# Three x tiles instead of four turned on TensorE, the fourth by the crossbar, and the gate weights loaded as five rows

## The chip, the cores and the metric

The kernel runs on one core of a Trainium2 chip. The time is device microseconds of that core. Each run lists a granted clock of 1.0 (1.0 is TensorE's full speed); that figure does not show the stretch at half speed that is found below (the page of before has 9, its top digit, in all 40 slices of that clock, and the first of them, 6.5 us long, holds the matmuls up to 3.7 us, which ran at half speed). A single profiled execution has a span 1.2 to 1.6 us shorter than the time that is quoted for it, because the time also holds what lies outside the profile.

## The reference, cut to what matters

```python
# x (2048, 640), wqkv (640, 1920), gate_w (640,)
g = sigmoid((x * gate_w).sum(-1, keepdims=True))
a = linear_attention(x @ wqkv) @ wo          # phi(q), phi(k): phi(t) = where(t > 0, t+1, exp(t)) + 1e-6
b = mixer_mlp(layernorm(x), w1, w2, w3, w4)
return g * a + (1 - g) * b
```

Only the first 20 us matter here: x comes in as 16 tiles of 128 tokens, each is turned (its features, in five slices of 128, become its rows) before TensorE multiplies it by the query and key weights, and `gate_w` rides along as one more column of the key weights, so that the gate's dot product costs no instruction of its own.

## The kernel before

The first four tiles are turned by TensorE (`t_x`, five 128x128 transposes each, then a copy on VectorE out of PSUM, the `ps` of the traces, into which TensorE writes). Tiles 4 to 15 are turned by a DMA that transposes on its way (DMA_TRANSPOSE in the traces; "through the crossbar" is its name here), which the SP queue issues after it has waited for the tile's 640 KB load. Query and key products come in "steps": one k (one of the five slices of 128 features) of one tile, a 512-column and a 128-column matmul.

```python
    dma_in(x_tok[:, 0, :], ...); dma_in(x_tok[:, 1, :], ...)      # cut
    load_wq(0)
    dma_in(x_tok[:, 2:4, :], x2[256:512, :]..., "x23")
    for k in range(1, KD): load_wq(k)
    for k in range(KD): dma_in(wkg[:, k, 0:D], ..., "wk%d" % k)
    dma_in(wkg[:, :, D + 2:D + 3], gate_w.rearrange("(k p o) -> p k o", p=128, o=1), "gw", noncontig=True)
    for c in range(1, NCH):
        dma_in(x_tok[:, 4 * c:4 * c + 4, :], ..., "xc%d" % c)
        for t in range(4 * c, 4 * c + 4):
            sch.dma("sp", xT[:, :, 128 * t:128 * (t + 1)], x_tok[:, t, :], "trx%d" % (t % 4), transpose=True)
    # ...
    WARM = 3200
    def t_x(t):
        tr_group(b, [x_tok[:, t, 128 * k:128 * (k + 1)] for k in range(KD)])   # cut: bank, src, dst
        copy(dve, dst, src)
    # ...
    def q_four():       # (tile, k); (tile, None) is t_x; (None, None) a short warm-up
        order = [(0, 0), (None, None), (1, 0), (2, None), (3, None), (0, 1), (1, 1), (2, 0), ...]
    # then k_first for tile 0, key tiles 1 to 3, and q, k of tile 4, 5, ...
```

A warm-up of 3,200 columns of matmul on a block of ones runs on TensorE while the first loads are under way.

## Time and profile before

| what | value |
|---|---|
| time | 260.96 us median of 3 (260.87 to 261.06) |
| TensorE (PE) busy | 255.7 of 259.6 us |
| PE's waits in all, after the first matmul | 0.8 us |
| first query step / first key step / query 4 | 5.06 / 11.80 / 17.27 us |
| crossbar transpose of tile 4 landed | 15.85 us |

From the page of before, the busy times, the granted clock in 40 slices, and the chain that ended last:

```profile
PE 255.7 (99%) x1690; PEld 132.2 (51%) x1690; DVE 151.7 (58%) x287; ACT 106.8 (41%) x216; POOL 92.8 (36%) x152
...
PEclk9999999999999999999999999999999999999999
...
PE 97%; DMA 1%; DVE 0%; SPq 0%; issue 0%
```

The whole kernel is one long stream of matmuls. Almost nothing is waited for, so what can be gained is TensorE work or one of the early waits. The early stretch is in the timeline of before (columns: start, busy time, engine, line, operation, tiles, count, and in brackets the idle time and what ended it):

```profile
3.69 0.75 PE L611 MATMUL ps<-ident,x_tok 128*128 128x128 bf16 x10
...
5.06 0.39 PE L874 MATMUL ps<-wq,xT 128*128 128x512 bf16 x1 [0.51 <-DMA wq<-in_A_wqkv_dram]
...
5.91 0.73 PE L611 MATMUL ps<-ident,x_tok 128*128 128x128 bf16 x10
6.48 0.38 PE L874 MATMUL ps<-wq,xT 128*128 128x512 bf16 x1
...
11.10 0.38 PE L874 MATMUL ps<-wq,xT 128*128 128x512 bf16 x1
11.31 0.22 PE L875 MATMUL ps<-wq,xT 128*128 128x128 bf16 x1
11.80 0.38 PE L874 MATMUL ps<-wkg,xT 128*128 128x512 bf16 x1 [0.27 <-issue]
```

Ten transposes take 0.57 us from the first to the next matmul (5.91 to 6.48). A query step takes 0.272 us, so the last one, started at 11.10, lets the next start at 11.37; the first key step starts at 11.80. The view says "issue", but the program makes this matmul wait for the gate load too. SP's timeline and the list of DMA issues (KB each, us to landing) give that load:

```profile
6.96 0.43 SPq L284 DMA_DIRECT2D wkg<-in_gate_w_dram  x1
wkg<-in_gate_w_dram SPq DMA_DIRECT2D x1, 1.2 KB, 4.7
```

Issued at 6.96, 4.7 us to landing: 11.7 us, for 1.2 KB. It came as 640 packets of 2 bytes, which started between 9.1 and 11.4 us, beside and behind the key weights.

### The profile page before, as it was taken

What the parts mean: (1) busy time and instruction counts of PE and PEld (TensorE: products, weight loads), DVE (VectorE), ACT (ScalarE), POOL (GpSimd) and SP (SyncE); (2) the same over time, 40 slices, a digit from 0 to 9 for tenths busy, and PEclk for the clock granted to TensorE, in tenths of its full rate; (3) what the DMA queues carried; (4) which work ended last, traced back from release to release, by engine and by line L of the source; (5) the groups of instructions that cost most, each with busy time, mean ns of one, the idle gap of its engine ahead of it and who ended that gap; (6) DMA issues with size and microseconds to landing.
All of it is one profiled execution on the core that took longest, in us unless ns stands there. A gap on an engine that the chain in (4) does not pass through costs nothing.

```text
span 259.6 us, 4300 instructions
## 1 busy us (share of the span) xinstructions
PE 255.7 (99%) x1690; PEld 132.2 (51%) x1690; DVE 151.7 (58%) x287; ACT 106.8 (41%) x216; POOL 92.8 (36%) x152
## 2 busy tenths in 40 slices
PE   7999999999999999999999999999999999999996
PEld 4555555554445454554444545554455544456453
DVE  1587887899902799999998407993033410143233
ACT  1496677751355766685854240005500045200000
POOL 4003995969863019667903202230011110021001
PEclk9999999999999999999999999999999999999999
DMA  6845969572656991752726650232000020000211
GB/s 195 260 104 146 198 176 143 167 139 44 110 108 123 352 337 36 72 101 52 105 56 124 124 61 0 41 85 78 0 3 0 3 101 0 0 3 1 104 51 51
DMA packets 51348, 24.99 MB, mean 96 GB/s; under 512 B 42708, under 2 KB 49917, under 8 KB 51328
## 3 DMA queue, kind: packets, MB, share of 16 engines
q1 hardware_dynamic: 49952, 21.31, 35.2%
q0 software_dynamic: 1136, 3.28, 5.8%
q8 instruction: 13, 0.21, 0.4%
q10 hardware_dynamic: 240, 0.13, 0.2%
q14 instruction: 7, 0.06, 0.1%
HBM read 12.05 MB, written 2.62 MB: 57 GB/s over the span
## 4 chain that ended last, share of the span: by engine, by line
PE 97%; DMA 1%; DVE 0%; SPq 0%; issue 0%
PE ps L600 61%; PE ps L1152 22%; PE ps L782 8%; PE ps L874 2%; DMA wq<-in_A_wqkv_dram 1%; PE ps L1064 1%; PE ps L1134 1%; PE ps L875 1%; DVE x_tok L639 0%; PE ps L954 0%; PE ps L983 0%; SPq L285 0%; PE ps L611 0%; PE ps L1131 0%; PE ps L847 0%
## 5 line engine op out<-in xcount | busy, mean ns | idle before, releaser
L600 PE MATMUL ps<-xnT,w 128*128 128x512 bf16 x360 | 81.5, 379 | 0.0
L1152 PE MATMUL ps<-w,h2T 128*128 128x512 bf16 (+1 forms) x416 | 58.8, 299 | 0.0
L656 ACT ACTIVATE h2T<-ps 128x512 bf16<-128x512 f32 x52 | 30.5, 598 | 67.5 <-PE ps L600 67.5
L600 PEld LDWEIGHTS ps<-xnT,w 128*128 128x128 bf16 x360 | 34.2, 98 | 38.5 <-issue 0.9
L639 DVE SCALAR_TENSOR_TENSOR x_tok<-ps,stg,abx 128x512 bf16<-128x512 f32 (+1 forms) x32 | 17.3, 550 | 61.5 <-PE ps L1152 61.5
L622 POOL TENSOR_SCALAR abx<-x_tok,stg 128x640 f32<-128x640 bf16 x16 | 14.8, 927 | 99.9 <-DVE x_tok L639 94.9
L1152 PEld LDWEIGHTS ps<-w,h2T 128*128 128x128 bf16 x416 | 32.2, 98 | 24.9 <-issue 1.1
L622 POOL TENSOR_SCALAR xn<-x_tok,st 128x640 bf16<-128x640 bf16 x32 | 34.4, 1082 | 14.3 <-DMA xnT<-xn 13.6
L656 ACT ACTIVATE Er<-ps 128x640 bf16<-128x640 f32 x32 | 22.5, 705 | 17.9 <-PE ps L600 8.5
L655 ACT ACTIVATE junk<-x_tok 128x640 bf16<-128x640 bf16 x32 | 23.6, 737 | 3.1 <-DVE x_tok L637 2.6
L600 PE MATMUL ps<-M_sb,pqnT 128*128 128x512 bf16 (+1 forms) x160 | 24.3, 299 | 0.0
L656 ACT ACTIVATE hsT<-ps 128x512 bf16<-128x512 f32 (+1 forms) x32 | 18.9, 594 | 13.0 <-PE ps L600 12.6
L600 PE MATMUL ps<-w,hsT 128*128 128x512 bf16 (+1 forms) x160 | 23.7, 299 | 0.0
L600 PE MATMUL ps<-wkg,xT 128*128 128x512 bf16 (+1 forms) x150 | 22.6, 299 | 0.0
L639 DVE SCALAR_TENSOR_TENSOR abx<-ps,stg,abx 128x640 f32<-128x640 f32 x16 | 14.1, 884 | 12.7 <-PE ps L600 11.7
L600 PEld LDWEIGHTS ps<-w,hsT 128*128 128x128 bf16 x160 | 13.3, 98 | 12.2
L600 PEld LDWEIGHTS ps<-M_sb,pqnT 128*128 128x128 bf16 x160 | 13.2, 98 | 10.9
L600 PE MATMUL ps<-wq,xT 128*128 128x512 bf16 (+1 forms) x120 | 18.3, 299 | 0.0
L782 PE MATMUL ps<-pk_tok,x_tok 128*128 128x512 bf16 x80 | 17.8, 379 | 0.0
L622 DVE TENSOR_SCALAR Er<-Er 128x640 bf16<-128x640 bf16 x32 | 11.6, 363 | 9.6 <-ACT Er L656 9.2
L637 DVE SCALAR_TENSOR_TENSOR x_tok<-ps,x_tok 128x640 bf16<-128x640 f32 x16 | 13.1, 820 | 6.4 <-PE ps L600 5.9
L600 PEld LDWEIGHTS ps<-wkg,xT 128*128 128x128 bf16 x150 | 12.2, 98 | 9.0
(75 smaller groups left out, 231.2 us busy)
## 6 DMA issues: line engine op xcount, KB each, us to landing
w<-in_B_w_dram SPq DMA_DIRECT2D x1, 2160.0 KB, 9.6
w<-in_B_w_dram SPq DMA_DIRECT2D x1, 2080.0 KB, 15.2
x_tok<-in_A_x_dram SPq DMA_DIRECT2D x3, 640.0 KB, 5.9
out_dram<-x_tok SPq DMA_DIRECT2D x3, 640.0 KB, 3.1
w<-in_B_w_dram POOLq DMA_DIRECT2D x8, 160.0 KB, 4.5
wq<-in_A_wqkv_dram SPq DMA_DIRECT2D x5, 160.0 KB, 3.6
wkg<-in_A_wqkv_dram SPq DMA_DIRECT2D x5, 160.0 KB, 4.3
wv<-in_A_wqkv_dram POOLq DMA_DIRECT2D x1, 800.0 KB, 5.9
```

Source lines behind the costliest of these rows:

```text
L600: ins = e.matmul(out_ap, l, r, start=(i == 0), stop=(i == n - 1))
L622: return engf(lambda e: e.tensor_scalar(out_ap, in_ap, s1, s2, op0, op1), rd, [out_ap], cost=cost)
L637: return dve(lambda e: e.scalar_tensor_tensor(out_ap, in0, scalar, in1, op0, op1, accum_out=accum), rd, [out_ap, accum], cost=cost + 70.0)
L639: return dve(lambda e: e.scalar_tensor_tensor(out_ap, in0, scalar, in1, op0, op1), rd, [out_ap], cost=cost)
L655: return act(lambda e: e.activation(out_ap, in_ap, func, bias=bias, scale=scale, accum_out=accum), rd, wr, cost=cost)
L656: return act(lambda e: e.activation(out_ap, in_ap, func, bias=bias, scale=scale), rd, wr, cost=cost)
L782: ins = e.matmul(o, l, r, start=(t0 + q_ == 0), stop=(t0 + q_ == NT - 1))
L874: e.matmul(ps[:, b, 0:512], l, w[:, k, 0:512], start=(k == 0), stop=(k == KD - 1))
L875: return e.matmul(ps[:, b + 1, 0:n2], l, w[:, k, 512:512 + n2], start=(k == 0), stop=(k == KD - 1))
L1064: ins = e.matmul(o, l, r, start=st, stop=sp)
L1134: ins = e.matmul(ps[:, bm, :], l, w4[rows, KFF, 0:512], start=True, stop=False)
L1152: ins = e.matmul(o, l, r, start=False, stop=(i == KFF - 1), skip_group_check=(n0 > 0))
```

## The change

The intent: take five transposes from TensorE (tile 3 goes through the crossbar, behind the keys of tiles 0 to 2), and bring `gate_w` in as five rows of 256 bytes, early and on another queue, into a zeroed 128-row block that one 5-column matmul turns into a column.

```diff
-    dma_in(x_tok[:, 2:4, :], ..., "x23")
+    dma_in(x_tok[:, 2, :], x2[256:384, :], "x2")
     for k in range(KD):
         dma_in(wkg[:, k, 0:D], ..., "wk%d" % k)
-    dma_in(wkg[:, :, D + 2:D + 3], gate_w..., "gw", noncontig=True)
+        if k == 2:
+            dma_in(x_tok[:, 3, :], x2[384:512, :], "x3")
+    gwr = xn[:, 1, 0:128]
+    dve(lambda e: e.memset(gwr, 0.0), [], [gwr])
+    sch.dma("act", xn[0:KD, 1, 0:128], gate_w.rearrange("(k p) -> k p", p=128), "gw")
     for c in range(1, NCH):
         dma_in(x_tok[:, 4 * c:4 * c + 4, :], ..., "xc%d" % c)
-        for t in range(4 * c, 4 * c + 4):
+        for t in range(3 if c == 1 else 4 * c, 4 * c + 4):
             sch.dma("sp", xT[...], x_tok[:, t, :], ..., transpose=True)
...
     def t_x(t):
+        if t == 2:
+            mm_group(ps[:, b, 448:448 + KD], [(gwr, ident[:, 0:KD])])
         copy(dve, dst, src)
+        if t == 2:
+            copy(dve, wkg[:, :, D + 1:D + 2], ps[:, b, 448:448 + KD]...)
...
-    q_four: order = [(0,0), warm, (1,0), tx2, tx3, (0,1), (1,1), (2,0), ...]; then k_first, key tiles 1 to 3
+    q_three: order = [(0,0), warm, (1,0), tx2, (0,1), (1,1), (2,0), ...]; then k_two (tiles 0, 1), key tile 2, query 3, key 3
-    key matmuls of 131 columns (two of ones, one of the gate)
+    key matmuls of 130 columns
```

(One POOL memset moved. From query 4 on the two programs have the same order on every engine.)

More of the change, by code (lines that the diff above doesn't have):

```diff
@@ L683, in _build @@
     load_wq(0)
-    dma_in(x_tok[:, 2:4, :], x2[256:512, :].rearrange("(n p) d -> p n d", p=128), "x23")
+    dma_in(x_tok[:, 2, :], x2[256:384, :], "x2")
     for k in range(1, KD):
@@ L688, in _build @@
         dma_in(wkg[:, k, 0:D], A_wqkv[128 * k:128 * (k + 1), D:2 * D], "wk%d" % k)
-    dma_in(wkg[:, :, D + 2:D + 3], gate_w.rearrange("(k p o) -> p k o", p=128, o=1), "gw", noncontig=True)
+        if k == 2:
[3 more added lines that the diff above has]
+    sch.dma("act", xn[0:KD, 1, 0:128], gate_w.rearrange("(k p) -> k p", p=128), "gw")
     for c in range(1, NCH):
         dma_in(x_tok[:, 4 * c:4 * c + 4, :], x2[512 * c:512 * (c + 1), :].rearrange("(n p) d -> p n d", p=128), "xc%d" % c)
-        for t in range(4 * c, 4 * c + 4):
+        for t in range(3 if c == 1 else 4 * c, 4 * c + 4):
             sch.dma("sp", xT[:, :, 128 * t:128 * (t + 1)], x_tok[:, t, :], "trx%d" % (t % 4), transpose=True)
@@ L727, in _build @@
     memset(pool, ones_c[:], 1.0)
+    memset(pool, wkg[:, :, D:D + 1], 1.0)
     aselect(ident[:], ones_c[:, 0:128], [[-1, 128]], ALU.is_equal, 0, 1)
-    memset(pool, wkg[:, :, D:D + 2], 1.0)
     memset(pool, negh[:], -0.5)
@@ L757, in t_x @@
         dst = xT[:, :, 128 * t:128 * (t + 1)]
+        if t == 2:
+            mm_group(ps[:, b, 448:448 + KD], [(gwr, ident[:, 0:KD])])
         copy(dve, dst, src)
+        if t == 2:
+            copy(dve, wkg[:, :, D + 1:D + 2], ps[:, b, 448:448 + KD].rearrange("p (k o) -> p k o", o=1))
     def phi(b, dst, after_exp=None):
@@ L772, in k_tile @@
         mm_group(ps[:, b, 0:512], [(xT[:, k, tok], wkg[:, k, 0:512]) for k in range(KD)])
-        mm_group(ps[:, b + 1, 0:131], [(xT[:, k, tok], wkg[:, k, 512:D + 3]) for k in range(KD)])
+        mm_group(ps[:, b + 1, 0:130], [(xT[:, k, tok], wkg[:, k, 512:D + 2]) for k in range(KD)])
         k_out(t, b)
@@ L879, in stream, with q_three, k_two @@
                 done(t, b)
-    def q_four():
-        order = [(0, 0), (None, None), (1, 0), (2, None), (3, None), (0, 1), (1, 1), (2, 0), (0, 2), (1, 2), (3, 0), (0, 3), (1, 3), (0, 4),
-                 (2, 1), (1, 4), (2, 2), (2, 3), (2, 4), (3, 1), (3, 2), (3, 3), (3, 4)]
+    def q_three():
+        order = [(0, 0), (None, None), (1, 0), (2, None), (0, 1), (1, 1), (2, 0), (0, 2), (1, 2), (2, 1), (0, 3), (0, 4),
+                 (1, 3), (2, 2), (1, 4), (2, 3), (2, 4)]
         stream(order, wq, 128, lambda t, b: phi(b, pq_tok[:, t + 1, :]))
     def k_out(t, b):
-        k_done[t] = phi(b, pk_tok[:, t, :], lambda: activation(lr[:, t, :], ps[:, b + 1, 129:131], ACTF.Copy))
+        k_done[t] = phi(b, pk_tok[:, t, :], lambda: activation(lr[:, t, :], ps[:, b + 1, 128:130], ACTF.Copy))
         activation(junk[:, 0, :], x_tok[:, t, :], ACTF.Square, accum=st1[:, 1, t:t + 1])
-    def k_first():
-        stream([(0, k) for k in range(KD)], wkg, 131, k_out)
+    def k_two():
+        stream([(0, 0), (0, 1), (0, 2), (1, 0), (0, 3), (1, 1), (1, 2), (0, 4), (1, 3), (1, 4)], wkg, 130, k_out)
     def addA(name, dur, fn, deps=()):
@@ L899, in _build @@
     addA(("warm", 1), 0.0, lambda: warmup(WARM2, 0.42))
-    addA(("q", 3), 5.44, q_four)
-    addA(("k", 0), 1.36, k_first)
-    for i in range(1, 4):
-        addA(("k", i), 1.36, lambda t=i: k_tile(t))
-    for i in range(4, NT + 2):
+    addA(("q", 2), 4.08, q_three)
+    addA(("k", 1), 2.72, k_two)
+    addA(("k", 2), 1.36, lambda: k_tile(2))
+    for i in range(3, NT + 2):
         if i < NT:
@@ L907, in _build @@
             addA(("k", i), 1.36, lambda t=i: k_tile(t))
-        for t in range(3) if i == 4 else (i - 2,):
-            addA(("g0", t), 0.27, lambda t=t: gt_tail(t), deps=[(("k", t), 2.0)])
+        if i > 3:
+            for t in range(3) if i == 4 else (i - 2,):
+                addA(("g0", t), 0.27, lambda t=t: gt_tail(t), deps=[(("k", max(t, 1)), 2.0)])
     IT.add("LW", ("lw1",), 0.0, load_w1, deps=[(("k", 5), 0.0)])
@@ L1231, in _build @@
     for t in range(NT):
-        deps = [(("zb",), 1.0), (("q", max(t, 3)), 2.0)]
+        deps = [(("zb",), 1.0), (("q", max(t, 2)), 2.0)]
         if t < 7:
```

## The prediction

> **What bounds the kernel.** TensorE. The page has PE busy 255.7 of 259.6 us (99%), full granted clock in all 40 slices, and the chain of waits is 97% PE; PE's own waits sum to 1.9 us, all before 12 us. A saving counts only if it shortens TensorE's stream or one of those early waits; then it should last to the end, for after the first few matmul groups both programs have the same order on every engine.
>
> **The early part before (timeline, landings).**
> - Ten transposes of tiles 2 and 3 start at 5.91, as their 320 KB landed at 5.86; PE was free at 5.73. They hold PE 0.57 us (57 ns each).
> - The 18 query steps after them run at 0.272 us each and end at 11.37. The first key matmul starts only at 11.80: 0.43 us lost. The page calls the gap "issue", but that matmul also waits for the gate_w load, which landed at 11.71, 1.08 us after the last key weights (10.63). The packets show why: 640 of 2 bytes between 9.2 and 11.5 us, DMA down to 114 GB/s. [...]
>
> **The change, costed.**
> 1. Five transposes leave PE: -0.285 us.
> 2. The gate load becomes five rows, early, on another queue; keys no longer wait for it: -0.43 us.
> 3. Tile 2 arrives alone, half the bytes: estimate 5.4 instead of 5.86, so its transposes start about 5.74: -0.17 us.
> 4. Key matmuls of 130 columns, not 131, 80 of them at about 0.4 ns a column: -0.03 us.
> 5. Added on PE: one 5-column matmul, about +0.06 us. Memset and 128x5 copy are on an idle DVE.
>
> All lies on PE's chain: -0.85 us if nothing new waits. By this sum queries 0-2 end at 9.65, keys 0-1 at 12.36, key 2 at 13.72, and query 4 starts at 16.4 instead of 17.27 (estimates).
>
> **New waits that may take some back.**
> - wq3 and wq4 landed at 8.05 and 8.46 and are now needed at 7.7 and 8.0. With 160 KB less ahead (0.44 us by the landings' spacing) they come at about 7.6 and 8.0: no slack, estimate 0.1 us lost.
> - Key tile 1 needs query 0's PSUM pair, free at 10.35 by the spacing of before, needed at 10.4.
> - Tile 3's crossbar transpose is issued when x3 lands (about 9.8). [...] it runs behind the 640 KB of tiles 4-7, clear about 12.2. Estimated landing 13.2, needed at 13.7. [...]
>
> I expect 0.15 us of these, net -0.7 us (0.3%): **260.25 us**, 8 in 10 between 259.9 and 260.8. Chances: faster by over 2% 0.005, within 2% 0.99, slower by over 2% 0.005.
>
> **What would show each step.** The first key matmul follows the last query matmul with no idle time (2); five transposes near 5.75 without the idle before them (1, 3); query 4 near 16.5 (sum); PE waits on wq, on the crossbar's xT or on DVE (new waits). From query 4 on everything stands 0.7 us earlier.
>
> **What would make it wrong.** The crossbar transpose landing after 14 us, so that PE waits at query 3 and the gain is gone, or a loss of up to 1 us; the first wq load delayed by the gate load or the later table load on ACT; the shift absorbed by a later wait without slack.

(Cut from the record: two rules about DMA that were quoted, not measured, and a sentence on a straggling DMA engine, which no run shows. No term of the sum is cut: items 1 to 5 still come to -0.85 us, and with 0.15 us of new waits to -0.7. That tile 3's transpose runs behind the 640 KB load, clear about 12.2, and lands at 13.2 thus stands as the author's estimate; in after that load landed at 13.52 and the transpose at 14.27. The 0.4 ns a column of item 4 is the query step's 0.272 us over its 640 columns. The 0.06 us of item 5 names no source; 0.03 was measured, in c2.)

## The result

| | time, us | ratio to before |
|---|---|---|
| before, 6 runs | 260.91 median (260.47 to 261.39) | |
| after, 6 runs | 260.81 median (260.68 to 261.05) | 0.9995 (0.9982 to 1.0008) |
| after again (a1), 5 runs | 261.14 median (260.79 to 261.82) | 1.0006 (0.9991 to 1.0020) |

A ratio here and below is the mean time of one kernel's fast runs over that of the other's of the same rounds, so not quite the ratio of the medians; the brackets are the 95% interval. Of the 0.7 us that was predicted nothing can be told from zero.

Lines of the page of after that answer to those of before:

```profile
PE 254.8 (98%) x1655; PEld 133.0 (51%) x1686; DVE 152.0 (59%) x288; ACT 106.5 (41%) x216; POOL 93.6 (36%) x152
...
PE 98%; issue 1%; DVE 0%; POOL 0%; POOLq 0%
```

Matmul records are missing from this trace (1,655 of 1,686), so the busy time does not say that TensorE worked less. This page has no row for the granted clock at all. The timeline of after over the same stretch:

```profile
3.69 1.27 PE L611 MATMUL ps<-ident,x_tok 128*128 128x128 bf16 x10
...
5.11 0.59 PE L882 MATMUL ps<-wq,xT 128*128 128x512 bf16 x1
...
5.81 0.63 PE L882 MATMUL ps<-wq,xT 128*128 128x512 bf16 x1
...
6.34 0.74 PE L611 MATMUL ps<-ident,x_tok 128*128 128x128 bf16 x5
6.88 0.21 PE L600 MATMUL ps<-ident,xn 128*128 128x5 bf16 x1
6.95 0.38 PE L882 MATMUL ps<-wq,xT 128*128 128x512 bf16 x1
...
7.44 0.22 PE L883 MATMUL ps<-wq,xT 128*128 128x128 bf16 x1
7.70 0.39 PE L882 MATMUL ps<-wq,xT 128*128 128x512 bf16 x1
...
10.64 0.22 PE L883 MATMUL ps<-wq,xT 128*128 128x128 bf16 x1
10.70 0.38 PE L882 MATMUL ps<-wkg,xT 128*128 128x512 bf16 x1
...
17.53 1.52 PE L600 MATMUL ps<-wq,xT 128*128 128x512 bf16 x10
```

Three things are to be seen.

1. The first key step follows the last query step without a gap (10.64, 10.70). That part of the change works as meant.
2. The same ten transposes at 3.69 took 1.27 us instead of 0.75, and the first 512-column query matmuls 0.59 and 0.63 instead of 0.39. From 6.95 on everything is as fast as before. **TensorE ran at half speed until 6.9 us here, and only until 3.7 us in the profile of before.** The starts of successive transposes tell it: 107 ns apart, which is called half speed here, or 56 ns, full speed. In a2 and b3 the change falls within this group of ten, which takes 1.15 and 0.88 us.
3. Between 7.44 and 7.70 a step is 0.2 us late; the view names no cause (b2 and c4 below find it).

The SP timelines of before and then of after show the crossbar transposes (DMA_TRANSPOSE), merged:

```profile
13.38 5.25 SPq L281 DMA_TRANSPOSE xT<-x_tok  x4
```

```profile
9.85 9.57 SPq L281 DMA_TRANSPOSE xT<-x_tok  x5
```

The individual landings, from the trace's landing records: in before tile 4 landed at 15.85, 1.4 us ahead of query 4 at 17.27. In after tile 3 landed at 14.27, and tile 4 at 17.45, 0.08 us ahead of query 4 at 17.53.

So there were two theories. **A**: the moment of full speed is drawn anew in each execution (it was 3.7 us in the profile of before and 6.9 in that of after), and a late draw costs the new kernel what it gained. **B**: tile 4's transpose now lands so late that TensorE could not have started query 4 sooner whatever happened before.

### The profile page after: what moved, and what is told of

Same layout as the page of the kernel before. It is cut to its first block, busy times and chain, and to the rows that moved or that the text cites. A ratio compares the mean times of both kernels' runs of the same rounds, so it can differ in the third digit from the quotient of the medians.

```text
span 259.8 us, 4263 instructions
## 1 busy us (share of the span) xinstructions
PE 254.8 (98%) x1655; PEld 133.0 (51%) x1686; DVE 152.0 (59%) x288; ACT 106.5 (41%) x216; POOL 93.6 (36%) x152
## 4 chain that ended last, share of the span: by engine, by line
PE 98%; issue 1%; DVE 0%; POOL 0%; POOLq 0%
PE ps L600 61%; PE ps L1160 21%; PE ps L790 8%; PE ps L882 2%; PE ps L855 1%; PE ps L1072 1%; PE ps L1142 1%; PE ps L883 1%; PE ps L611 1%; DVE x_tok L639 0%; PE ps L962 0%; PE ps L991 0%; PE ps L1139 0%; POOL xn L659 0%; POOLq L1306 0%
## 5 line engine op out<-in xcount | busy, mean ns | idle before, releaser
L600 PE MATMUL ps<-xnT,w 128*128 128x512 bf16 x348 | 80.4, 379 | 0.7 <-issue 0.2
L600 PE MATMUL ps<-M_sb,pqnT 128*128 128x128 bf16 (+1 forms) x156 | 23.6, 297 | 0.3
L600 PE MATMUL ps<-wkg,xT 128*128 128x130 bf16 (+1 forms) x138 | 21.1, 298 | 0.1
L600 PE MATMUL ps<-wq,xT 128*128 128x128 bf16 (+1 forms) x128 | 19.7, 298 | 0.1
L600 PEld LDWEIGHTS ps<-M_sb,pqnT 128*128 128x128 bf16 x160 | 13.2, 98 | 10.8
L1101 DVE TENSOR_TENSOR pq_tok<-pq_tok,dnr 128x300 bf16<-128x300 bf16 (+1 forms) x48 | 16.8, 403 | 0.6
```

What stands on the lines that cost most here:

```text
L600: ins = e.matmul(out_ap, l, r, start=(i == 0), stop=(i == n - 1))
L1101: dve(lambda e, o=o, i0=i0, i1=i1: e.tensor_tensor(o, i0, i1, ALU.mult), [i0, dnr[:, 1, sd, :]], [o], cost=cost)
```

## The experiments

Twelve kernels ran, all with the right result, in three groups of four; those of one group ran on one chip and share the runs of before; the groups ran on three different chips. From query 4 on nothing differs but one column, so one number of a profile tells the rest: the start of the first product of x with the keys (the "tail product", which follows key 4). Time of the profiled run minus this start lay between 240.79 and 240.97 us in all eleven profiles of this table, so the start is the time up to 0.2 us.

| kernel | full speed from | first key step | waits from there to the tail product | tail product | time of this run |
|---|---|---|---|---|---|
| before | 3.74 | 11.80 | 0 | 20.00 | 260.84 |
| a2, before again | 4.58 | 11.50 | 0 | 19.70 | 260.57 |
| b4, before, early warm-up | 5.5 | 11.47 | 0 | 19.67 | 260.64 |
| a3, gate part alone | 3.73 | 11.98 | 0 | 20.16 | 261.01 |
| c2, gate part, early warm-up | 5.6 | 11.61 | 0 | 19.79 | 260.59 |
| after | 6.9 | 10.70 | 0 | 20.25 | 261.05 |
| a1, after again | 6.9 | 10.69 | 0.79 | 21.03 | 261.82 |
| a4, after, tile 4 loaded alone | 6.9 | 10.70 | 0 | 20.25 | 261.06 |
| c1, after, early warm-up | 4.88 | 9.87 | 0.54 | 19.96 | 260.77 |
| b3, both | 3.97 | 10.06 | 0 | 19.61 | 260.41 |
| c3, both, copy cut in two | 6.8 | 10.39 | 0 | 19.94 | 260.73 |

"Full speed from" is read from the trace's clock record where there is one and else from the spacing of the matmuls. "Waits" is the tail product's start minus that of the first key step, less 8.20 us in the kernels that turn four tiles on TensorE (six tile products and no wait) and less 9.55 in the others (seven). The profiles of b1, b2 and c4 are left out of the table: there time minus this start is 241.17, 241.04 and 241.08.

### a1 and a2: the two kernels again

No edit.

> The changed kernel unaltered, for a second profile and more times. Theory A (the start of full TensorE speed falls at a random time): in the profile of after, matmuls ran at half speed until about 6.9 us, in that of before only until 3.7 us; the moment should differ again here, and the start of query 4 should follow it: near 16.5 if full speed starts before 4.5 us, near 17.5 if after 6.5 us. Theory B (tile 4's crossbar transpose caps the gain): query 4 does not start before its xT lands (17.45 in the profile of after), whatever the speed; with an early full speed TensorE shows an idle gap before query 4 of 0.3 to 1 us.

> The kernel before, unaltered, as a control and for a second profile. Ratio 1.000 within 0.001. Theory A: the first half-speed stretch ends anywhere between 3.6 and 7 us, and a late end puts the start of query 4 up to 1 us later than 17.27. If it is again near 3.7 and the times of both kernels spread alike, theory A does not explain the lost gain.

a1: 261.14 us (260.79 to 261.82), ratio 1.0006. a2: 260.75 (260.57 to 261.45), ratio 0.9998 (0.9984 to 1.0012). In a1 full speed came late again, at 6.9, and this time theory B's wait is in the profile. The list of TensorE's waits and the timeline of a1:

```profile
PE ps L600 <- DMA xT<-x_tok: 0.6, 1, 0.6
```

```profile
16.16 1.53 PE L600 MATMUL ps<-wkg,xT 128*128 128x512 bf16 x10
18.30 1.53 PE L600 MATMUL ps<-wq,xT 128*128 128x512 bf16 x10 [0.61 <-DMA xT<-x_tok]
```

Key 3 would have let query 4 start at 17.52; it started at 18.30, when tile 4's transpose had landed at 18.25. This is the slowest run of the eleven of after. Theory B's wait is shown, and it can come even with a late full speed.

a2 shows something else. Its gate load landed at 11.41 and its first key step started at 11.50:

```profile
11.18 0.22 PE L875 MATMUL ps<-wq,xT 128*128 128x128 bf16 x1
11.50 0.38 PE L874 MATMUL ps<-wkg,xT 128*128 128x512 bf16 x1
```

The query steps alone give 11.24: this gap is 0.26 us, not 0.43. In b4's profile the load landed at 11.19, before the query steps ended, and there is no gap at all.

a2 also limits theory A. Its full speed came 0.84 us later than in before, and yet its query 4 started at 16.97, 0.30 us earlier, not later. The same holds for b4 and c2 (full speed at 5.5 and 5.6, query 4 at 16.94 and 17.06). In before TensorE waited for weights until 5.06 and for tiles 2 and 3 until 5.91, so slow work ahead of those waits need not cost anything. No profile with four tiles on TensorE has a start as late as 6.9.

### a3: the gate part alone

```diff
 (before, with:)
-    dma_in(wkg[:, :, D + 2:D + 3], gate_w..., "gw", noncontig=True)
+    memset of gwr, five rows on the ACT queue, 5-column matmul and 128x5 copy in t_x(2), 130 key columns
```

> Before with only the gate part of the change (five rows, zeroed block, one 5-column matmul, 130 key columns); all four tiles still turned on TensorE. If the 2-byte gate load cost 0.43 us of TensorE time, the first key matmul follows the last query matmul without a gap, and the time is 0.3 to 0.45 us below before (ratio about 0.9985), for the crossbar of tile 4 has slack (landed 15.85, needed 17.27 in before). Rival: the gap is given back in a later wait, ratio 1.000.

261.01 us (260.77 to 261.38), ratio 1.0001 (0.9990 to 1.0013): the expected 0.3 to 0.45 us is not there. The first key step follows the last query step at once, at 11.98. But in this profile tiles 2 and 3 landed at 6.42 instead of 5.86, and the timeline of a3 has the wait one step earlier:

```profile
6.47 0.45 PE L611 MATMUL ps<-ident,x_tok 128*128 128x128 bf16 x5 [0.49 <-DMA x_tok<-in_A_x_dram]
```

The gap before the keys stood in series with other loads that vary by half a microsecond from run to run. That this edit made the load late is not shown: in c2, with the same edit, tiles 2 and 3 landed at 5.92. The rival (the gap is given back in a later wait) is neither shown nor refuted: the loss in this profile came before the gap, not after it.

### a4: tile 4 loaded by its own transfer

```diff
 (after, with:)
+        if c == 1:
+            dma_in(x_tok[:, 4, :], x2[512:640, :], "x4")
+            dma_in(x_tok[:, 5:8, :], x2[640:1024, :]..., "xc1")
```

> After, but tile 4 of x is loaded by its own 160 KB transfer ahead of tiles 5 to 7, so its crossbar transpose need not wait for the whole 640 KB. Theory B: its transpose is issued at about 11.7 instead of 13.5 us, lands near 14.5 instead of 17.45, query 4 starts right behind key 3, and the time drops 0.3 to 0.7 us below after. Theory A alone: no difference from after beyond 0.1 us.

The mechanism did what was expected: tile 4's transpose was issued at 11.18 and landed at 14.24, 3.3 us before it was needed. The time did not move in the median, 260.90 us, but the six runs spread from 260.12 to 262.61 (two of them, 260.12 and 260.23, as fast as b3 below), ratio 0.9999 (0.9974 to 1.0023). The profile explains its own run: full speed only from 6.9, first key at 10.70, no wait after it, query 4 at 17.53, and 261.06 us. So even without theory B's wait the gain is gone in this profile, by the late full speed and by 0.21 us that b2 finds: the cap was not the only thing in the way. The slow outlier and the two fast runs have no profile.

### b1 and b2: all real work held back until full speed is sure

```diff
 (before, and after, with:)
-    memset(pool, ones_c[:], 1.0)
+    for _ in range(8):
+        memset(pool, ones_c[:], 1.0)     # the identity for the transposes comes behind these
-    WARM = 3200
+    WARM = 7168
```

> The kernel before, with all real TensorE work held back to about 7 us by seven more memsets ahead of the identity and 7,168 instead of 3,200 warm-up columns, so that TensorE is at full speed before its first transpose whenever that speed starts (3.7 to 7.0 us). Theory A (the moment of full speed scatters the times): the spread of the times falls from about 0.9 us to under 0.35 us. Time about 2.3 us above before: transposes at 7.05 instead of 3.7, but no wait for any wq, x or gate load afterwards. Rival (scatter comes from elsewhere, such as late loads): spread stays about 0.9 us.

> The changed kernel with the same delay. Query 4 then starts near 20 us, well after tile 4's crossbar transpose (17.5 to 18.3 us), and no load is waited for; what is left of the change is five transposes less on TensorE, one 5-column matmul more, one column less: 0.25 us below b1, to the end of the kernel, with a spread under 0.35 us. If it is not below b1, TensorE time saved here is given back later, which no theory so far says.

b1: 264.33 us, five runs within 264.33 to 264.34. b2: 264.17 us, 264.17 to 264.20. (The work started at 7.75 instead of the expected 7.05, which is 0.7 of the microsecond by which both are longer than expected.) The scatter of 0.9 us and more that before shows beside them (260.69 to 262.23) is gone. That shows that it arises in the first 7.75 us, but not which of the two things the hold-back removes made it: both a late full speed and a late first load are hidden by it. Full speed started at 3.69 in the profile of b1 and at 6.91 in that of b2, with no effect on the work behind.

The second result is a surprise: b2 is 0.16 us faster than b1, not 0.25. The timeline of b1, where every load is long there and full speed reigns, and then those of b2, TensorE's and VectorE's:

```profile
9.52 0.72 PE L611 MATMUL ps<-ident,x_tok 128*128 128x128 bf16 x10
...
10.62 0.38 PE L875 MATMUL ps<-wq,xT 128*128 128x512 bf16 x1
```

```profile
10.10 0.38 PE L883 MATMUL ps<-wq,xT 128*128 128x512 bf16 x1
10.31 0.22 PE L884 MATMUL ps<-wq,xT 128*128 128x128 bf16 x1
10.58 0.39 PE L883 MATMUL ps<-wq,xT 128*128 128x512 bf16 x1
```

```profile
10.03 0.49 DVE L665 COPY xT<-ps 128x640 bf16<-128x640 bf16 x1 [0.91 <-PE ps L600]
```

The step of b2 at 10.58 should have started at 10.37. It is query 2's first, and it needs tile 2's turned x, which VectorE copies out of PSUM after the transposes, here from 10.03 to 10.52. b1's step at 10.62 is the same one, and nothing delays it. In before five more transposes (those of tile 3) stood between the transposes of tile 2 and this step; now only two steps do. In the two profiles the tail product is only 0.04 us apart (23.17 and 23.13). The transposes that were taken away had been covering a copy. From the tail product to the last matmul b2 is another 0.04 us shorter (237.29 to 237.33 us), as step 4's missing column would make it. So TensorE's stream explains about 0.08 of the 0.16 us; the rest lies outside the profiled span (1.59 us in b1, 1.49 in b2) and has no known cause.

### c4: the same with the copy of tile 2 cut in two

```diff
 (b2, with, in t_x:)
-        copy(dve, dst, src)
+        for k0, k1 in ((0, 2), (2, KD)) if t == 2 else ((0, KD),):
+            copy(dve, dst[:, k0:k1, :], src[:, k0:k1, :])
```

> b2 with the same cut copy, where times repeat within 0.03 us. If the removed transposes uncovered the copy, the time drops by 0.15 to 0.21 us from 264.17 to about 264.0, which then is 0.3 us below b1: the TensorE time that the prediction counted. Rival: no change, 264.17.

263.98 us (263.98 to 264.02), 0.19 below b2 and 0.35 below b1. It ran on another chip than those two, so the profile is the firmer witness. The timeline of c4:

```profile
10.11 0.38 PE L884 MATMUL ps<-wq,xT 128*128 128x512 bf16 x1
10.32 0.22 PE L885 MATMUL ps<-wq,xT 128*128 128x128 bf16 x1
10.39 0.39 PE L884 MATMUL ps<-wq,xT 128*128 128x512 bf16 x1
```

The step starts at 10.39 instead of 10.58, and the tail product at 22.94 instead of 23.13: 0.19 us, all of which arrives at the end. The wait was the copy.

### b3 and b4: an earlier warm-up

```diff
 (a4, and before, with:)
-    memset(pool, xn[:, 0, 0:128], 1.0)          # the warm-up's operand
-    WARM = 3200
+    WARM = 3456
-    e.matmul(..., xn[:, 0, 0:128], xn[:, 0, 0:128]...)
+    e.matmul(..., nc.const_aps.tensor(1.0, [128, 128], BF16), nc.const_aps.tensor(1.0, [128, n], BF16))
```

> The x4 split, with the warm-up matmuls on a constant that the preamble has written, so that they start 0.25 us earlier (0.80 instead of 1.05), 256 more columns. [...] Then full speed from about 3.5 us in the profile, query 4 near 16.5 us, and 260.2 us in the median (0.7 below before). Rival: the profile shows half speed until 6.9 us again, and the time is that of the x4 split, 260.9.

> The kernel before with only the earlier warm-up. Its three profiles (this one, a2, a3 family) already had full speed from 3.7 to 4.6 us, so: same as before, ratio 0.9985 to 1.0, fewer runs above 261.3.

b3: 260.34 us (260.14 to 260.85), ratio 0.9968 (0.9950 to 0.9985), clearly faster than before on the same chip. b4: 260.90 (260.55 to 261.40), ratio 0.9987 (0.9971 to 1.0004), not told from before. The warm-up started at 0.83 instead of 1.05. In b3's profile full speed came at 3.97 (3.5 was expected), the first query step had to wait for its weights until 5.33, and no wait followed. Tile 4's transpose landed at 14.49.

```profile
5.33 0.39 PE L885 MATMUL ps<-wq,xT 128*128 128x512 bf16 x1 [0.68 <-DMA wq<-in_A_wqkv_dram]
...
6.00 0.44 PE L611 MATMUL ps<-ident,x_tok 128*128 128x128 bf16 x5
...
10.06 0.38 PE L885 MATMUL ps<-wkg,xT 128*128 128x512 bf16 x1
```

Five transposes take 0.27 us here (6.00 to the next matmul at 6.27) against 0.54 in after. This is about the kernel that was predicted.

### c1, c2, c3: which part of b3 did it

c1 is after with only the earlier warm-up, c2 the gate part (a3) with it, c3 is b3 with the copy cut in two; no edits beyond those shown.

> The changed kernel with only the earlier warm-up, no split of the 640 KB load. Theory B: with full speed by about 4 us TensorE reaches query 4 near 16.5 us but tile 4's crossbar transpose lands at 17.4 to 18.3, so TensorE idles 0.5 to 1.5 us there and the time is 0.4 to 0.8 us above that of c3 or b3 (260.34), that is 260.7 to 261.2. Rival (the early warm-up alone made b3 fast): 260.3, no idle time before query 4.

> Before with the gate part and the earlier warm-up; tile 3 still turned on TensorE, nothing on the crossbar before tile 4. It lacks the removed transposes, but also the new waits. If the gate part is worth what the gap before the first key matmul showed (0.1 to 0.43 us in two profiles of before), it is 0.1 to 0.4 us below b4 (260.9), near 260.6, and above b3.

> b3 with the copy of tile 2's turned x out of PSUM cut in two (k 0 to 1, then 2 to 4), so that query 2's first matmul waits for the first piece only. In after, a1, a4, b2 and b3 that matmul started 0.21 us late behind this copy. Expect the gap gone and about 0.2 us below b3: 260.15, the fastest version, 0.3% below before. Rival: the gap is wq2 or the bank, and the time is b3's.

c1: 260.92 us (260.41 to 261.12), ratio 0.9995 (0.9982 to 1.0007). The time is in theory B's range, but its profile corrects the theory. Full speed came at 4.88 and the first key step at 9.87, 0.83 earlier than in after. Then 0.54 us went, and not to tile 4, which had landed at 16.57. The timeline of c1:

```profile
12.11 0.39 PE L881 MATMUL ps<-wkg,xT 128*128 128x512 bf16 x1 [0.15 <-DMA wkg<-in_A_wqkv_dram]
...
12.94 1.53 PE L600 MATMUL ps<-wkg,xT 128*128 128x512 bf16 x10
14.51 1.53 PE L600 MATMUL ps<-wq,xT 128*128 128x512 bf16 x10
...
17.24 1.03 PE L600 MATMUL ps<-wq,xT 128*128 128x512 bf16 x4
```

The last key weights landed at 12.06, and the step that needs them, which the steps before it allowed at about 11.80, started at 12.11. A key tile takes 1.36 us, so query 3 could have started at 14.30; tile 3's transpose landed at 14.47, and it started at 14.51. So at an early full speed TensorE outran two other loads first. What theory B says of tile 4 holds of the whole queue: key weights 4, tile 3 and tile 4 are all close to TensorE's need.

c2: 260.95 us (260.59 to 261.14), ratio 0.9998 (0.9986 to 1.0011): again nothing for the gate part alone, against the expected 0.1 to 0.4 us.

c3: 260.50 us (260.15 to 260.81), ratio 0.9982 (0.9970 to 0.9995). Faster than before a second time, on another chip, but not faster than b3 as expected. In its profile full speed came only at 6.8, in spite of the earlier warm-up, and still its first key step came at 10.39, 0.31 before that of after. The cut copy's 0.19 us, which c4 shows, is smaller than the scatter of the start.

### What holds the transposes up

Two further things were read in all profiles rather than tried. First, in each one an instruction fetch of 16 KB (a queue of its own, kind "instruction", 13 in the whole kernel) passes once between 13 and 18.2 us. In before and a2 it fell at 13.2 us, ahead of the first crossbar packet, and all four transposes landed 2.5 to 2.6 us after their issue. In after (15.36 us), a1 (14.88), a3 (13.83), a4 (15.78), b1 (16.27), b2 (18.12), b3 (14.16), c3 (14.89) and c4 (17.34) one transpose that was in flight then landed 3.7 to 4.6 us after its issue: about 19 or 20 of its 256-byte packets, which take 18 ns in the median, took from 0.5 to 1.9 us where they were looked at (after, a1, a3, a4). In the remaining three (b4 at 13.26, c2 at 13.56, c1 at 13.87) it began 0.1 to 0.9 us after the issue of tile 4's transpose, which landed 2.8 to 3.3 us after its issue: the same pattern, smaller. Where it fell on tile 4 (after, a1, a3) that tile came late; where tile 4 had been issued earlier (a4, b3, c3) it fell on a later tile that had slack. The coincidence is there in nine profiles, and weaker in three, but no run moved the fetch, so the cause is argued, not shown. Second, tile 3's packets in after and a1 stood up to 1.5 and 1.8 us among those of the 640 KB load, whose landing (13.52 and 13.82) was not earlier than in before (13.36), although the 2-byte packets were gone. The prediction had it clear at 12.2, by an estimate. The order was as predicted (the transpose landed after that load, at 14.27 and 14.57), the times were not.

## Why the prediction was right or wrong

The time lies at the edge of the stated range (260.81, range to 260.8) and "within 2%" is right. Neither credits the mechanism: without any gain the time would have been 260.9, only 0.1 us away, which is less than the runs scatter. The forecast gain of 0.7 us is wrong: six and five runs show none. Point by point:

- **"TensorE bounds the kernel, and a saving lasts to the end": right.** Time minus the start of the tail product is 240.8 to 241.0 us in the eleven profiles of the table (241.0 to 241.2 in b1, b2 and c4), and c4's 0.19 us arrived whole.
- **Step 1, five transposes, -0.285: the work is right, the credit wrong.** Five take 0.27 us at full speed. But "all lies on PE's chain" failed: they had hidden the copy of tile 2, and 0.21 us came back as a wait behind VectorE (b2: the tail product 0.04 us earlier than b1; c4: 0.19 more once the copy is cut). The prediction called that engine idle and did not ask what its latency stood behind.
- **Step 2, the gate load, -0.43: mechanism right, size taken from one profile.** The gap is 0.43, 0.26 and 0 us in three profiles of before (before, a2, b4), and alone it brought nothing that the times show (a3, c2).
- **Step 3, tile 2 alone, 5.4 instead of 5.86: right** (5.25 and 5.47 in after and a1). In those two TensorE was still at half speed then and could not use it.
- **Steps 4 and 5: right, and small.** With 130 columns the stretch from the tail product to the last matmul is 237.29 us, with 131 it is 237.33 in before and b1 (a2 and b4 have further delays there). The 5-column matmul holds TensorE for 0.03 us at full speed (0.06 was predicted): in c2 it starts at 6.28 and the next transpose at 6.31.
- **The sum, first key step at 9.65: nearly right where its premise held.** In c1, with full speed at 4.88, it is 9.87: 9.65 and the 0.21 of the copy. (In b3, with 3.97, it is 10.06, for its first weights landed 0.26 us later than in before.)
- **The premise that failed: that TensorE's speed from 3.7 us on is part of the kernel.** It was read from one profile. In after full speed came at 6.9 us, and the first key step 0.83 us later than in c1, which is after with only the earlier warm-up. (No run set the moment of full speed, so what it costs is read from profiles, not shown by times.) Neither the sum nor the list of what could go wrong had this.
- **The new waits, 0.15 us: too small.** They cost 0.79 us in a1 and 0.54 us in c1, and none in after, whose late start hid them. "The crossbar transpose landing after 14 us" was named: it landed at 14.27 and 14.57. But the transpose that hurt most was the next one, tile 4, which the prediction did not list; its slack of 1.4 us was eaten from both sides.

What replaces the prediction: by its sum, about 0.85 us of room is made in front of query 4. Of this the uncovered copy takes 0.21 at once. If full speed comes as late as 6.9, that takes another 0.83. If it comes early, TensorE runs into the loads of the last key weights, tile 3 and tile 4. In after and c1 it so reached query 4 within 0.3 us of before (17.53 and 17.24 against 17.27); in a1 a late full speed and the wait for tile 4 came together, and query 4 started at 18.30, 1.0 us later than in before. A kernel that loads tile 4 alone and starts the warm-up earlier has the gain, at 260.34 (b3) and, with the copy cut in two, 260.50 us (c3): 0.3% and 0.2% below before, and the best that was found. That the earlier warm-up brings full speed sooner is not shown: in the five profiles that have it, it came at 4.0, 4.9, 5.5, 5.6 and 6.8.

What stays open: whether the change itself makes a late full speed likelier. In the four profiles that start the warm-up at 1.05 us and turn four tiles on TensorE (before, a2, a3, b1) it came at 3.7 to 4.6 us, in the five that start it there and turn three (after, a1, a4, b2, c4) at 5.4 to 6.9. Such a split by chance has a probability of 1 in 126, but no cause is known: TensorE's program is the same until then. With the earlier warm-up the split is not there (5.5 and 5.6 with four tiles, 4.0, 4.9 and 6.8 with three). What sets off full speed is not shown either: it came 2.6, 4.4 and 5.9 us after the first matmul in b1, c4 and b2, whose warm-up ran without a break until then, and no run set its moment. And b3's gain is not split between its two edits: each alone (a4, c1) showed none, on two chips.

## What to carry to other kernels

Before costing a saving of a few tenths of a microsecond at the start of a kernel, take several profiles: what looked like a property of the kernel (a 0.43 us gap, a fast first microsecond) was one draw. When work is taken off the bounding engine, ask what its duration was covering on the other engines and queues, and give those their head start in the same edit. And where times scatter, hold the work back until the disturbance is over: two versions that could not be told apart at 0.9 us of scatter repeated within 0.03 us and showed their 0.16 us (read the profile beside it: half of that was not TensorE's work).
